# Packed attention and SwiGLU on one core: in the later batches, one output product ahead of M and the attention products

## The chip, the cores and the metric

The kernel runs on one core of one Trainium2 chip. The metric is device time in microseconds (us) of one execution. Engines are named as in the profile: PE is the TensorE with its matmuls, PEld its weight loads, DVE the VectorE, ACT the ScalarE, POOL the GpSimd, SP the queue that issues the DMAs.

## The reference

Two attentions in a row, of which the second has the output of the first as keys and values, and then a gated feed-forward layer over all tokens. There are 8 batches, 8 heads, 576 positions, 64 elements a head, 32 packed rows, model width 512 and inner width 1536.

```python
def sm_attn(qq, kk, vv):
    s = scale * np.matmul(qq, kk.transpose(0, 1, 3, 2))
    s = s - np.max(s, axis=-1, keepdims=True)
    a = np.exp(s)
    a = a / (np.sum(a, axis=-1, keepdims=True) + 1e-09)
    return np.matmul(a, vv)
p_packed = sm_attn(p, k, v)
out = sm_attn(q, p_packed, p_packed)
...
g = x @ w_gate              # x: out, as 4608 tokens x 512
silu = g * (1.0 / (1.0 + np.exp(-g)))
val = x @ w_val
return (silu * val @ w_out).astype(np.float32)
```

## The kernel before

The kernel doesn't form x. The second attention's weights a2 (tokens by 32 packed rows of each head) are multiplied by M, which is the packed output of the first attention times w_gate and w_val. M is made anew for each batch, in parts of two chunks of the inner width; a chunk is 128 of its 1536 columns, so there are 12 chunks (`fc` 0 to 11) in a batch. Each factor of these products, and of the output product, is split into a high and a low part (`mh`/`ml`, `a2h`/`a2l`, `hh`/`hl`, `wo_h`/`wo_l`), and three of the four products of parts are added up in PSUM.

The first batch follows a written program of its own. The later batches (b = 1 to 7) go through `batch(b, behind)`. A chunk there does this on PE: gate/value of its first half (256 tokens), the output products of the preceding chunk's first half, gate/value of its second half (320 tokens), the output products of the preceding chunk's second half. Gate/value (`gv_chunk`, L655) is 12 matmuls, six into each of two PSUM banks; ACT reads the first bank (silu, L662) and DVE the second (L666, and L669 for 64 tokens that are kept apart), then the product is split (`hh`, `hl`). An output product (`out_mm`, L674) is three matmuls of 512 columns into one of four accumulators. A half has two of them (`c` = 0 and 1, for 128 tokens each).

PE's order is the order in which the program is written. `fill`, called after each bank of gate/value and after each output product, counts up in the chunk, and `run(fc, place)` issues what a table has for that place: the next batch's attention, piece by piece. At count 2, when gate/value of the first half is issued, a chunk of odd number also issues a part of M (`m_part`, L274 into two `aux` banks). The pieces at place "ha" come right after: the first attention's scores (`q_scores`, L416), its packed product (`q_pack`, L500) or the second attention's scores (`s2_mm`, L274 with `q_t`). These go into the pool `gv`, which has two banks and is the pool of gate/value too, so the next gate/value takes the banks that they leave. DVE reads them: the scores by a maximum and a subtraction a bank (L431, L432), the packed product by eight small transposes (L512), the second attention's scores by one transpose a bank (L533). Behind those reads DVE makes `hl` (L636) and the low parts of M (L593).

The odd chunks of batches 1 to 6 carry scores in chunk 1, pack in 5, second scores in 7 and 9, and, in batches 1 to 5, scores again in 11. Chunk 3 has M alone, as have chunk 11 of batch 6 and the odd chunks of batch 7 up to 9.

DVE, ACT and SP follow the order that a scheduler finds, except for instructions that are pinned to the order of the program.

Of the kernel before, what the change touches and what calls it, by code (L numbers as in the profile page):

```python
# [20 lines left out]
B, H, S, D = 8, 8, 576, 64  # L21
NP = 32
DM, DF = 512, 1536
P = 128
NPAR, NHP = 2, 4
NFC = DF // P
# [108 lines left out]
def tile_pack_attention_swiglu(ctx: ExitStack, tc: tile.TileContext, qT, kT, v, vq, pT, wgv, wout, out):  # L135
# [96 lines left out]
    def wout_high(fc):  # L232
        k, i = divmod(fc, 2)
        if i == 0:
            wo_h[k], wo_l[k] = pair(F32R, "wo_h"), pair(F32R, "wo_l")
        pin(nc.scalar.copy(wo_h[k][:, i], wos[k][:, i]))

    def wout_low(fc):
        k, i = divmod(fc, 2)
        pin(nc.vector.tensor_tensor(wo_l[k][:, i], wos[k][:, i], wo_h[k][:, i].bitcast(F32), op=ALU.subtract))  # L240
# [350 lines left out]
    def m_lows():  # L591
        while lows:
            pin(nc.vector.tensor_tensor(*lows.pop(0), op=ALU.subtract))  # L593
# [29 lines left out]
    def m_part(b, k, fcs):  # L623
        m_mm(b, k, fcs)
        m_high(b, k, fcs)
# [6 lines left out]
    def h_split(src, hi, lo, between=lambda: False, tag=""):  # L632
        hh, hl = (pool.tile([P, 256], F32R, tag=t + tag, bufs=2, name=t) if tag else h_tile(t) for t in ("hh", "hl"))
        copy(hi, hh, src)
        last = between()
        low = lo.tensor_tensor(hl, src, hh.bitcast(F32), op=ALU.subtract)  # L636
        if last:
            pin(low)
        return hh, hl

    def gv_chunk(b, fc, is_b, fill, behind, between):
        odd = b % 2
        n = NB if is_b else NA
        off = (0 if odd else 256) if is_b else (320 if odd else 0)
        mh, ml = ms[b, fc // 2]
        ah, al = a2[b]
        f = fc % 2
        pgs = []
        for s in range(2):
            pg = ps_gv.tile([P, 512], F32, tag="gv", name="gv")  # L650
            pgs.append(pg)
            i = 0
            for m_, a_ in ((ml, ah), (mh, al), (mh, ah)):
                for g in range(NPAR):
                    nc.tensor.matmul(  # L655
                        pg[:, :n], m_[:, g, f, s * P : (s + 1) * P], a_[:, g, off : off + n],
                        start=(i == 0), stop=(i == 5),
                    )
                    i += 1
            fill()  # L660
        sg = pool.tile([P, NB], F32, tag="sg", bufs=1, name="sg")
        nc.scalar.activation(sg[:, :n], pgs[0][:, :n], AF.Silu)  # L662
        behind()
        hf = pool.tile([P, 256], F32, tag="hf", bufs=2, name="hf")
        o, o4 = (64, 0) if is_b and odd else (0, 256)
        nc.vector.tensor_tensor(hf, pgs[1][:, o : o + 256], sg[:, o : o + 256], op=ALU.mult)  # L666
        if is_b:
            r, r4 = slice(64 * odd, 64 * odd + 64), slice(o4, o4 + 64)
            nc.vector.tensor_tensor(t4[b // 2][:, fc, r], pgs[1][:, r4], sg[:, r4], op=ALU.mult)  # L669
        return h_split(hf, nc.scalar, nc.vector, between)  # L670

    def out_mm(acc, hh, hl, c, fc, at=slice(0, DM), first=False):
        for i, (h_, w_) in enumerate(((hl, wo_h), (hh, wo_l), (hh, wo_h))):
            nc.tensor.matmul(  # L674
                acc[:, at],
                h_[:, c : c + P],
                w_[fc // 2][:, fc % 2, at],
                start=((fc == 0 or first) and i == 0),
                stop=(fc == NFC - 1 and i == 2),
            )  # L680
# [58 lines left out]
    def plan_of(b):  # L739

        plan = {}
        for d in (b + 1, b + 2):
            if d >= B:
                continue
            for line in table_of(d).strip().splitlines():
                place, *todo = line.split()
                fc, place = place.split(".")
                fc = int(fc) + NFC * (d - b - 1)
                if (0 if d > 2 else -NFC) <= fc < NFC:
                    plan.setdefault((fc, int(place) if place.isdigit() else place), []).extend((words2[w], d) for w in todo)  # L750
        return lambda fc, place: bool([f(d) for f, d in plan.pop((fc, place), ())])

    with tc.manual_schedule(engines={mybir.EngineType.PE}):
# [8 lines left out]
        def accs_of(b):  # L762
            odd = b % 2
            row0 = (b // 2) * 2 * S
            rows = [row0 + P * t for t in ((7, 8, 5, 6) if odd else (0, 1, 2, 3))]
            return rows, [ps_acc.tile([P, 512], F32, tag="acc", name="acc") for _ in range(4)]

        def t4_of(b):
            t4[b // 2] = pool.tile([P, NFC * P + 48], F32, tag="t4", bufs=1, name="t4")[:, : NFC * P].rearrange(
                "p (f t) -> p f t", f=NFC  # L770
            )

        with tc.manual_schedule(
# [18 lines left out]
            rows, accs = [], []  # L792
# [133 lines left out]
        def last_outs(rows, accs, out):  # L926
            def last(which):
                out(which)
                for c in range(2 * which, 2 * which + 2):
                    emit_out(accs[c], rows[c], c % 2)  # L930

            return last
# [4 lines left out]
        def batch(b, behind):  # L937
            if not b % 2:
                t4_of(b)
            run = plan_of(b)  # L940
            ha, hb = {}, {}
            accs, rows = [], []

            def outs(fc, which, fill=lambda: None):
                src = (hb if which else ha).pop(fc)
                for c in range(2):
                    out_mm(accs[2 * which + c], *src, c * P, fc)
                    fill()

            for fc in range(NFC):  # L950
                count = [0]

                def fill():
                    count[0] += 1
                    if count[0] == 2:
                        run(fc, 2)
                        if fc == NFC - 1 and b + 1 < B:
                            m_part(b + 1, 0, both)
                        elif fc % 2 and fc + 1 < NFC:
                            m_part(b, (fc + 1) // 2, both)  # L960
                    if b == 1 and 1 <= fc <= 2 * SPLIT - 4 and count[0] == 7:
                        wout_high(fc + 3)
                        wout_low(fc + 3)
                    if count[0] != 2:
                        run(fc, count[0])

                ha[fc] = gv_chunk(b, fc, False, fill, lambda: run(fc, "a"), lambda: run(fc, "ha"))
                m_lows()
                if fc:
                    outs(fc - 1, 0, fill)  # L970
                else:
                    behind(0)
                hb[fc] = gv_chunk(b, fc, True, fill, lambda: run(fc, "b"), lambda: run(fc, "hb"))
                if fc:
                    outs(fc - 1, 1, fill)
                else:
                    behind(1)
                    for x, y in zip((rows, accs), accs_of(b)):
                        x.extend(y)
            last = last_outs(rows, accs, lambda which: outs(NFC - 1, which))  # L980
            if not b % 2:
                return last
            p4, halves = [], {}

            def split4(*ks):
                for k in ks:
                    halves[k] = h_split(
                        t4_t[:, 2 * k : 2 * k + 2].rearrange("p f t -> p (f t)"), nc.vector, nc.vector, tag="4"
                    )

            def mm4(*ks):
                for k in ks:
                    for i in range(2):
                        out_mm(p4[0], *halves[k], i * P, 2 * k + i)

            def behind_p4(which):
                if which == 0:
                    p4.append(ps())
                    for k in range(4):
                        mm4(k)  # L1000
                        split4(k + 2)
                else:
                    row = (b // 2) * 2 * S + 4 * P
                    if b == B - 1:
                        mm4(4)
                        end_out(p4[0], row, halves[5])
                        return
                    mm4(4, 5)
                    emit_out(p4[0], row, 0)

            t4_t = t4.pop(b // 2)
            split4(0, 1)
            for which in range(2):
                last(which)
            return behind_p4

        for b in range(1, B):
            behind = batch(b, behind)
# [40 lines left out]
```

## Time and profile before

| | |
|---|---|
| median of 3 timed runs | 728.88 us (728.43 to 729.27) |
| span of the profiled execution (its own time, first to last instruction; the page has no other) | 727.1 us |
| the median over that span | 1.8 us |
| mean granted TensorE clock | 1.000 |
| PE gate/value, L655, on the chain that ended last | 37% |
| PE output products, L674 into `acc`, on that chain | 36% |
| M and the second attention's scores, L274 into `aux`, on that chain | 7% |

A row of the timeline gives start, duration, engine, line, operation and tiles (output<-inputs), the count of instructions that it merges, and in brackets the idle time of the engine ahead of it with what ended it. Durations of matmuls reach to a modelled end and overlap with the next one; the step from one start to the next tells what a matmul took of PE. A 32-bit matmul that isn't split stands in the trace as two, so M's 8 instructions are 16 rows and the scores' 16 are 32. Rows of waits give what waited, for whom, the total in us, how often, and the longest.

### The profile page before, as it was taken

What the parts mean: (1) busy time and instruction counts of PE and PEld (TensorE: products, weight loads), DVE (VectorE), ACT (ScalarE), POOL (GpSimd) and SP (SyncE); (2) the same over time, 40 slices, a digit from 0 to 9 for tenths busy, and PEclk for the clock granted to TensorE, in tenths of its full rate; (3) what the DMA queues carried; (4) which work ended last, traced back from release to release, by engine and by line L of the source; (5) the groups of instructions that cost most, each with busy time, mean ns of one, the idle gap of its engine ahead of it and who ended that gap; (6) DMA issues with size and microseconds to landing.
All of it is one profiled execution on the core that took longest, in us unless ns stands there. A gap on an engine that the chain in (4) does not pass through costs nothing.

```text
span 727.1 us, 14219 instructions
## 1 busy us (share of the span) xinstructions
PE 715.4 (98%) x5768; PEld 588.9 (81%) x5768; DVE 466.4 (64%) x1061; ACT 374.6 (52%) x675; POOL 2.0 (0%) x13
## 2 busy tenths in 40 slices
PE   6899999999999999999999999999999999999998
PEld 3656788888888888888888888888888888888886
DVE  5998999665745657565665566666574655744333
ACT  3889855734635355552653526653553535433331
POOL 0000000000000000000000000000000000000000
PEclk9999999999999999999999999999999999999999
DMA  9887293220212201302112021102001000010002
GB/s 356 313 301 280 94 372 108 89 73 1 67 72 72 74 1 66 128 3 73 66 59 85 3 73 67 59 4 73 1 2 73 5 1 1 1 60 1 1 1 73
DMA packets 20145, 59.10 MB, mean 81 GB/s; under 512 B 6000, under 2 KB 7280, under 8 KB 17520
## 3 DMA queue, kind: packets, MB, share of 16 engines
q1 hardware_dynamic: 19792, 57.96, 22.1%
q8 instruction: 46, 0.75, 0.4%
q10 hardware_dynamic: 288, 0.23, 0.1%
q14 instruction: 19, 0.16, 0.1%
HBM read 48.69 MB, written 9.49 MB: 80 GB/s over the span
## 4 chain that ended last, share of the span: by engine, by line
PE 96%; DVE 1%; ACT 0%; issue 0%; ACTq 0%; DVEq 0%
PE gv L655 37%; PE acc L674 36%; PE aux L274 7%; PE gv L821 6%; PE aux L674 5%; PE acc L862 3%; PE gv_aux L500 1%; PE gv_aux L274 1%; PE gv_aux L416 1%; PE acc L760 0%; PE aux L361 0%; DVE s L548 0%; DVE r L547 0%; PE gv_aux L361 0%; PE aux L342 0%; DVE s L533 0%
## 5 line engine op out<-in xcount | busy, mean ns | idle before, releaser
L662 ACT ACTIVATE sg<-gv 128x256 f32<-128x256 f32 (+1 forms) x168 | 69.1, 411 | 173.7 <-PE gv L655 161.6
L666 DVE TENSOR_TENSOR hf<-gv,sg 128x256 f32<-128x256 f32 x168 | 70.8, 422 | 120.0 <-PE gv L655 108.4
L674 PE MATMUL acc<-wo_h,hl 128*128 128x512 f32 x360 | 146.5, 407 | 0.0
L655 PE MATMUL gv<-a2h,ml 128*128 128x256 f32 (+1 forms) x672 | 143.7, 295 | 0.0
L655 PE MATMUL gv<-a2l,mh 128*128 128x256 f32 (+1 forms) x672 | 143.4, 295 | 0.0
L655 PE MATMUL gv<-a2h,mh 128*128 128x256 f32 (+1 forms) x672 | 143.4, 295 | 0.0
L674 PE MATMUL acc<-wo_l,hh 128*128 128x512 f32 x360 | 141.8, 394 | 0.0
L674 PE MATMUL acc<-wo_h,hh 128*128 128x512 f32 x360 | 141.8, 394 | 0.0
L655 PEld LDWEIGHTS gv<-a2h,ml 128*128 128x128 f32 x672 | 116.3, 189 | 15.1
L185 ACT CAST hh<-hf 128x256 fp32r<-128x256 f32 x168 | 67.7, 403 | 104.0 <-DVE hf L666 103.9
L655 PEld LDWEIGHTS gv<-a2l,mh 128*128 128x128 f32 x672 | 107.7, 189 | 0.1
L655 PEld LDWEIGHTS gv<-a2h,mh 128*128 128x128 f32 x672 | 107.6, 188 | 0.0
L636 DVE TENSOR_TENSOR hl<-hf,hh 128x256 fp32r<-128x256 f32 x168 | 70.0, 417 | 46.3 <-ACT hh L185 45.9
L674 PEld LDWEIGHTS acc<-wo_h,hl 128*128 128x128 f32 x360 | 67.5, 188 | 30.4 <-issue 20.3
L674 PEld LDWEIGHTS acc<-wo_h,hh 128*128 128x128 f32 x360 | 67.6, 188 | 15.3
L674 PEld LDWEIGHTS acc<-wo_l,hh 128*128 128x128 f32 x360 | 67.7, 188 | 8.7 <-ACT mh L619 0.2
L593 DVE TENSOR_TENSOR ml<-aux,mh 128x512 fp32r<-128x512 f32 x92 | 58.9, 681 | 3.7 <-ACT mh L619 3.4
L274 PE MATMUL aux<-w,ppt 64*32 64x512 f32 (+1 forms) x784 | 52.1, 588 | 0.0
L619 ACT CAST mh<-aux 128x512 fp32r<-128x512 f32 x92 | 49.4, 590 | 5.0 <-PE aux L274 0.5
L662 ACT ACT_TABLE_LOAD x30 | 38.5, 1283 | 14.0 <-PE gv L655 9.5
L205 ACT ACTIVATE st<-st,minus_two 128x1024 f32<-128x1024 uint32 x18 | 22.6, 1264 | 0.0
L862 PE MATMUL acc<-wo_f,h 128*128 128x512 f32 x48 | 22.5, 601 | 0.0
(158 smaller groups left out, 743.8 us busy)
## 6 DMA issues: line engine op xcount, KB each, us to landing
st<-in_wgv SPq DMA_DIRECT2D x12, 1024.0 KB, 6.5
k_t<-in_kT SPq DMA_DIRECT2D x16, 576.0 KB, 4.8
q_t<-in_qT SPq DMA_DIRECT2D x16, 576.0 KB, 5.0
out<-ot SPq DMA_DIRECT2D x35, 256.0 KB, 2.1
v_t<-in_vq SPq DMA_DIRECT2D x6, 1280.0 KB, 5.8
st<-in_wout SPq DMA_DIRECT2D x6, 1024.0 KB, 6.2
v_t<-in_v SPq DMA_DIRECT2D x2, 1024.0 KB, 8.3
p_t<-in_pT SPq DMA_DIRECT2D x7, 64.0 KB, 2.4
```

What stands on the lines that cost most here:

```text
L185: e.copy(dst, src)
L205: yield nc.scalar.activation(lo.bitcast(F32), lo.bitcast(U32), AF.Identity, bias=minus_two, scale=LOW_WORD)
L274: nc.tensor.matmul(outs[par][32 * hp : 32 * hp + 32], lhs(r, hp), rhs(r, hp), start=True, stop=True)
L593: pin(nc.vector.tensor_tensor(*lows.pop(0), op=ALU.subtract))
L619: nc.scalar.copy(m[0][at], src)
L636: low = lo.tensor_tensor(hl, src, hh.bitcast(F32), op=ALU.subtract)
L655: nc.tensor.matmul(pg[:, :n], m_[:, g, f, s * P : (s + 1) * P], a_[:, g, off : off + n], start=(i == 0), stop=(i == 5),)
L662: nc.scalar.activation(sg[:, :n], pgs[0][:, :n], AF.Silu)
L666: nc.vector.tensor_tensor(hf, pgs[1][:, o : o + 256], sg[:, o : o + 256], op=ALU.mult)
L674: nc.tensor.matmul(acc[:, at], h_[:, c : c + P], w_[fc // 2][:, fc % 2, at], start=((fc == 0 or first) and i == 0), stop=(fc == NFC - 1 an ...
L821: nc.tensor.matmul(held[i][s][:, :n], m_[:, g, f, s * P : (s + 1) * P], a_[:, g, off : off + n], start=(j == 0), stop=(j == len(todo) - 1),)
L862: nc.tensor.matmul(accs[2 * is_b + c], half(i)[:, c * P : c * P + P], wos[fc // 2][:, fc % 2], start=(fc == 0), stop=(fc == NFC - 1),)
```

## The change

In an odd chunk, once gate/value of the first half is issued and before M, the first of the two output products of the preceding chunk's first half is issued (`c` = 0, into `accs[0]`). It is noted in `early`, and `outs` leaves it out where it stood. M and the attention pieces at "ha" follow, then the second output product, then gate/value of the second half as before. The last chunk of the last batch is left as it was. That is 41 places: 6 in each of batches 1 to 6 and 5 in batch 7.

```diff
+            early = set()
+
             def outs(fc, which, fill=lambda: None):
                 src = (hb if which else ha).pop(fc)
                 for c in range(2):
-                    out_mm(accs[2 * which + c], *src, c * P, fc)
+                    if (fc, which, c) not in early:
+                        out_mm(accs[2 * which + c], *src, c * P, fc)
                     fill()
...
                     if count[0] == 2:
                         run(fc, 2)
+                        if fc % 2 and (fc + 1 < NFC or b + 1 < B):
+                            early.add((fc - 1, 0, 0))
+                            out_mm(accs[0], *ha[fc - 1], 0, fc - 1)
                         if fc == NFC - 1 and b + 1 < B:
                             m_part(b + 1, 0, both)
                         elif fc % 2 and fc + 1 < NFC:
```

PE at chunk 1 of a batch, before (`gv` is gate/value, `aux<-w` is M, `gv_aux<-k_t` the scores, `acc` the output products):

```order
L655 MATMUL gv<-a2h,mh 128x256 x2
L274 MATMUL aux<-w_82,ppt 32x512 x8
L416 MATMUL gv_aux<-k_t,p_t 32x144 x16
L674 MATMUL acc<-wo_h,hl 128x512
L674 MATMUL acc<-wo_l,hh 128x512
L674 MATMUL acc<-wo_h,hh 128x512
L674 MATMUL acc<-wo_h,hl 128x512
L674 MATMUL acc<-wo_l,hh 128x512
L674 MATMUL acc<-wo_h,hh 128x512
L655 MATMUL gv<-a2h,ml 128x320 x2
```

The same place on PE now:

```order
L655 MATMUL gv<-a2h,mh 128x256 x2
L674 MATMUL acc<-wo_h,hl 128x512
L674 MATMUL acc<-wo_l,hh 128x512
L674 MATMUL acc<-wo_h,hh 128x512
L274 MATMUL aux<-w_82,ppt 32x512 x8
L416 MATMUL gv_aux<-k_t,p_t 32x144 x16
L674 MATMUL acc<-wo_h,hl 128x512
L674 MATMUL acc<-wo_l,hh 128x512
L674 MATMUL acc<-wo_h,hh 128x512
L655 MATMUL gv<-a2h,ml 128x320 x2
```

Three matmuls of an output product moved ahead of M and the scores; three instead of six stand between the scores and gate/value's second half.

PE at chunk 5, before (`gv_aux<-v_t` is the packed product):

```order
L655 MATMUL gv<-a2h,mh 128x256 x2
L274 MATMUL aux<-w_84,ppt 32x512 x8
L500 MATMUL gv_aux<-v_t,a_1643 32x64 x40
L674 MATMUL acc<-wo_h,hl 128x512
L674 MATMUL acc<-wo_l,hh 128x512
L674 MATMUL acc<-wo_h,hh 128x512
L674 MATMUL acc<-wo_h,hl 128x512
L674 MATMUL acc<-wo_l,hh 128x512
L674 MATMUL acc<-wo_h,hh 128x512
L655 MATMUL gv<-a2h,ml 128x320 x2
```

The same place on PE now:

```order
L655 MATMUL gv<-a2h,mh 128x256 x2
L674 MATMUL acc<-wo_h,hl 128x512
L674 MATMUL acc<-wo_l,hh 128x512
L674 MATMUL acc<-wo_h,hh 128x512
L274 MATMUL aux<-w_84,ppt 32x512 x8
L500 MATMUL gv_aux<-v_t,a_1643 32x64 x40
L674 MATMUL acc<-wo_h,hl 128x512
L674 MATMUL acc<-wo_l,hh 128x512
L674 MATMUL acc<-wo_h,hh 128x512
L655 MATMUL gv<-a2h,ml 128x320 x2
```

Here too one output product went ahead of M and the packed product, and one stayed behind it.

ACT, SP and POOL keep their order. On DVE a few neighbours change places; the one that recurs is in chunk 3, shown as a difference (`ml` are M's low parts, `y`, `x` and `z` the first attention's maxima and sums):

```order
 L636 TENSOR_TENSOR hl<-hf,hh 128x256
-L593 TENSOR_TENSOR ml<-aux,mh 128x512 x2
-L460 TENSOR_REDUCE y_1555<-x_1487 128x8
-L461 TENSOR_TENSOR y_1555<-x_1487,y_1555 128x32
-L464 TENSOR_TENSOR y_1555<-z_1273,y_1555 128x8
+L593 TENSOR_TENSOR ml<-aux,mh 128x512
+L460 TENSOR_REDUCE y_1558<-x_1487 128x8
+L593 TENSOR_TENSOR ml<-aux,mh 128x512
+L461 TENSOR_TENSOR y_1558<-x_1487,y_1558 128x32
+L464 TENSOR_TENSOR y_1558<-z_1273,y_1558 128x8
```

The small maximum now stands between the two low parts of M instead of behind them.

## The prediction

> **What bounds the kernel now.** I read the page's busy and clock rows first, then the waits of PE (the TensorE), then the waits of DVE (the VectorE) that the change touches, and last the timeline around the moved products. Two lines of the page:
>
> ```profile
> PE 715.4 (98%) x5768; PEld 588.9 (81%) x5768; DVE 466.4 (64%) x1061; ACT 374.6 (52%) x675; POOL 2.0 (0%) x13
> PEclk9999999999999999999999999999999999999999
> ```
>
> PE fills 98% of the span, at an undisturbed clock. Busy PE says little by itself, since ends of matmuls are modelled, so the waits decide. All that PE's own view of the waits lists is this (what waited, for whom, us in total, times, longest):
>
> ```profile
> PE acc_aux L274 <- DMA p_t<-in_pT: 4.9, 1, 4.9
> PE gv L821 <- DVE a2f L790: 1.3, 1, 1.3
> PE gv L821 <- ACT mh L619: 0.8, 1, 0.8
> PE gv_aux L361 <- DMA v_t<-in_v: 0.7, 1, 0.7
> PE gv L821 <- ACT sg L837: 0.5, 1, 0.5
> ```
>
> Each belongs to the first batch's program (L821, L361, L274 on the first load). In the later batches, where the change acts, PE is never listed as waiting. So there is nothing for a reordering of PE to recover there, unless a wait hides in a matmul's duration; every slip of a result that PE needs soon can only cost. Who reads the moved products, and how ready it is, is in the waits of DVE:
>
> ```profile
> DVE s L533 <- PE gv_aux L274: 12.8, 12, 1.1
> DVE z L431 <- PE gv_aux L416: 11.6, 11, 1.1
> DVE ppt L512 <- PE gv_aux L500: 10.7, 6, 1.8
> ```
>
> DVE stands idle over 1 us in front of every attention product and starts when PE ends it. If PE ends it later, DVE starts later by as much. The counts give the sites: 11 of scores (L416), 6 of pack (L500), 12 of the second attention product (L274 with q_t), all in chunks of odd number. A further 12 odd chunks have M alone.
>
> **The score sites.** Timeline of PE and DVE at chunk 1 of a middle batch (start, duration, engine):
>
> ```profile
> 388.57 0.40 PE L655 MATMUL gv<-a2h,mh 128*128 128x256 f32 x2
> 388.90 1.09 PE L274 MATMUL aux<-w,ppt 64*32 64x512 f32 x16
> ...
> 389.78 0.75 PE L416 MATMUL gv_aux<-k_t,p_t 64*32 64x144 f32 x32
> ...
> 390.46 0.50 PE L674 MATMUL acc<-wo_h,hl 128*128 128x512 f32 x1
> 390.80 0.40 PE L674 MATMUL acc<-wo_l,hh 128*128 128x512 f32 x1
> 391.03 0.40 PE L674 MATMUL acc<-wo_h,hh 128*128 128x512 f32 x1
> 391.06 0.46 DVE L432 TENSOR_TENSOR e<-gv_aux,z 128x288 f32<-128x288 f32 x1
> 391.26 0.40 PE L674 MATMUL acc<-wo_h,hl 128*128 128x512 f32 x1
> ...
> 391.91 0.46 DVE L432 TENSOR_TENSOR e<-gv_aux,z 128x288 f32<-128x288 f32 x1
> 391.95 0.46 PE L655 MATMUL gv<-a2h,ml 128*128 128x320 f32 x2
> ...
> 392.84 0.45 PE L655 MATMUL gv<-a2h,ml 128*128 128x320 f32 x2
> ```
>
> One output product is three matmuls: the second one runs from 391.26 to the start of gate/value's second half at 391.95, 0.69 us. The first, now ahead of M, pushes M and the scores back by 0.69 and leaves only the second between the scores and gate/value. The work of PE up to gate/value is unchanged, so without waits gate/value would still be due at 391.95. But the scores use both banks of the two-bank gv pool, and gate/value needs the first of them back. DVE gives it back at 391.06 + 0.46 = 391.52, 0.43 before it is due. Slipped by 0.69 that is 392.21, 0.26 too late, and a bank given back isn't used at once: for that time the pack site has the row.
>
> **The pack sites.** Pack takes one bank, which gate/value needs for its second bank, half-way through:
>
> ```profile
> 418.07 2.06 DVE L512 STREAM_TRANSPOSE ppt<-gv_aux 32x64 f32<-32x64 f32 x8 [1.81 <-PE gv_aux L500]
> ...
> 420.02 0.46 PE L655 MATMUL gv<-a2h,mh 128*128 128x320 f32 x2
> 420.31 0.50 PE L655 MATMUL gv<-a2h,ml 128*128 128x320 f32 x2
> 420.65 0.46 PE L655 MATMUL gv<-a2l,mh 128*128 128x320 f32 x2
> ```
>
> Eight transposes end at 418.07 + 2.06 = 420.13, and the matmul that needs their bank starts 0.18 later, exactly when it is due (pairs follow each other by 0.29). The next pair then starts 0.34 later instead of 0.29: the bank came just in time, and 0.05 was lost since the second weight load was late too. So pack has no slack at all. I take 0.18 as the time from release to matmul, and 0.05 as the extra after a wait.
>
> Price per pack site: the whole slip, 0.69 (its 0.05 is paid already). Six of them: 4.1 us. Price per score site: 0.69 + 0.18 - 0.43 = 0.44, with the 0.05 it is 0.49; eleven: 5.4 us. The second bank adds nothing: it is free at 391.91 + 0.46 + 0.69 + 0.18 = 393.24, and with the wait it is due at 392.84 + 0.49 = 393.33. The lower bound, a bank used as soon as it is released, is 0.26 a site, 2.9 in all.
>
> **The second attention product.** Here DVE needs one transpose per bank, from the group's mean 463 ns; after it come M's low halves, a maximum (L547) and the multiplication that ends gate/value (L666, L669):
>
> ```profile
> L533 DVE STREAM_TRANSPOSE s<-gv_aux 128x288 f32<-128x288 f32 x26 | 11.1, 463 | 13.2 <-PE gv_aux L274 12.8 <-PE acc_aux L274 0.4
> ```
>
> ```profile
> 431.74 0.85 DVE L533 STREAM_TRANSPOSE s<-gv_aux 128x288 f32<-128x288 f32 x2 [1.06 <-PE gv_aux L274]
> ...
> 432.82 1.28 DVE L593 TENSOR_TENSOR ml<-aux,mh 128x512 fp32r<-128x512 f32 x2
> ...
> 433.07 0.46 PE L655 MATMUL gv<-a2h,ml 128*128 128x320 f32 x2
> ...
> 434.01 0.74 DVE L547 TENSOR_REDUCE r<-s 128x18 f32<-128x576 f32 x1
> ...
> 435.10 0.43 DVE L666 TENSOR_TENSOR hf<-gv,sg 128x256 f32<-128x256 f32 x1 [0.35 <-PE gv L655]
> ...
> 436.11 0.22 DVE L669 TENSOR_TENSOR t<-gv,sg 128x64 f32<-128x64 f32 x1
> 436.22 0.40 PE L655 MATMUL gv<-a2h,ml 128*128 128x256 f32 x2
> ...
> 436.93 0.40 PE L655 MATMUL gv<-a2h,ml 128*128 128x256 f32 x2
> ```
>
> The first bank is free at 431.74 + 0.46 = 432.20; with slip and latency 433.07, exactly when it is due. I take 0 and keep 0.07 a site (0.8 in all) for the upper end. DVE itself stays 0.69 late here, as PE didn't wait: L547 ends at 434.01 + 0.74 + 0.69 = 435.44, so L666 starts 0.34 late, and L669 frees its bank at 436.33 + 0.34 + 0.18 = 436.85, against 436.93. Covered, by 0.08; that cover is thin, and what it costs if gone is a rival below.
>
> **What costs nothing.** M alone (12 sites): no gv bank is read there, and M's low halves, ready at 432.82 + 1.28 = 434.10 even at the crowded site, have until the next chunk at 436.22; that slack of 2.1 also covers the small maximum (L460) that now stands between the two of them in chunk 3 of some batches. The product moved forward needs the low half of the chunk before. It is latest ahead of chunk 11:
>
> ```profile
> 455.44 0.42 DVE L636 TENSOR_TENSOR hl<-hf,hh 128x256 fp32r<-128x256 f32 x1
> ...
> 457.33 0.66 PE L274 MATMUL aux<-w,ppt 64*32 64x512 f32 x8
> ```
>
> It is there at 455.86, and the place where M stands now comes at 457.33: 1.4 to spare. DMAs keep their order on SP, and POOL's clearing of e is issued as before; the sums whose maxima SP gathers stand a chunk later, by when DVE has waited for PE again.
>
> **The boundary in front of M.** PE changes from full 128-row products to 64-row ones once per site, before as after, but behind a 512-wide matmul instead of a 256-wide one. Before: last 256-wide start 388.69 (388.57 + 0.12), M 388.90: 0.21, that is 0.09 over the usual 0.12. A wider one stands in the first batch:
>
> ```profile
> 80.24 0.46 PE L821 MATMUL gv<-a2h,ml 128*128 128x320 f32 x2
> ...
> 80.63 0.66 PE L274 MATMUL aux<-w,ppt 64*32 64x512 f32 x8
> ```
>
> The second of the pair starts at 80.39 (spacing 0.15), M 0.24 later: again 0.09 over. So it doesn't depend on the width: 0.
>
> **Sum.** 5.4 + 4.1 = 9.5 us on the profiled execution's span of 727.1: 736.6. The timed runs' median, 728.88, lies 1.8 above that span; with the same margin 738.4. Bounds of the costs: 2.9 + 4.1 = 7.0 and 9.5 + 0.8 = 10.3, so 735.9 to 739.2 if the mechanism holds.
>
> **Rivals.**
> DVE's lag bites at the second product. If L548, which stands between L666 and L669, delays the release by the full slip of 0.69 instead of 0.34, the bank comes 0.27 late, 12 times: 3.2 us more, 741.6. Against it: L666 had 0.35 of idle time that absorbs half the slip.
>
> The boundaries get cheaper (the other side). M's 0.09 might belong to the narrow product in front of it, and the slow start of the first output product behind the tiles (390.46 to 390.80, 0.34, where the next step, 390.80 to 391.03, takes 0.23: 0.11) might go as well. Both gone at 41 sites would give back 0.20 x 41 = 8.2, leaving 1.3: 730.2, within noise. It decides from 0.23 a site. Only the first half gone: 3.7, 734.7. For it: the order in front of M really changes. Against it: the 320-wide row above, and the second output product still comes right behind tiles.
>
> PE's clock drops because PE now stops 17 times.
>
> ```profile
> 20.00:25.00 5.00, 3.69 (x19) 2.98 (x18) 4.92 (x9) 4.01 (x7) 0.00 (x0) 1.00 0.91 366
> ```
>
> ```profile
> 23.49 0.45 PE L821 MATMUL gv<-a2f,mh 128*128 128x256 f32 x1 [1.31 <-DVE a2f L790]
> ```
>
> The granted clock (1.00 in the first row) stayed full over a gap of 1.31 us, longer than any stop here, so I give it little. If the gate/value half behind each stop (1.76 us, the 0.88 from 391.95 to 392.84 twice) ran at half clock, it would add 17 x 1.76 = 30: 768. The Trainium skill ("TensorE: Matmul & The Clock Gate", section "A second HAM failure mode: psum-queue depth-cycling") tells of a kernel whose short idle times between groups, while cycling through PSUM banks, made the clock oscillate; the row above doesn't show it here.
>
> The change does nothing: the slip is smaller than 0.25 at the scores only if PE starts M under the first output product. M's start after the last full product, 0.09 late, speaks against that. It would leave 728.9.
>
> **Chances.** Mechanism as summed 0.79; DVE's lag on top 0.08; boundary rival 0.06, half of it to no change and half to 734.7; the change does nothing 0.01; clock 0.03; faster by something unseen 0.03, since PE's waits could be hidden in modelled ends. Slower 0.93, same 0.04, faster 0.03, with 0.2% (1.5 us) as what a measurement can tell. The range 735.2 to 741.7 takes in the lag rival and the bounds.
>
> **What would show it.** Right: PE waits listed on DVE's L432 (11, some 0.4 each) and L512 (6, some 0.7), in front of L655, or first matmuls of that line later by as much; DVE's idle time in front of the three readers grows by what PE gained; the first 512-wide pair to M some 0.31 apart. Wrong: no gap at gate/value behind scores and pack, M starting closer than 0.25 behind the wide product, or a clock row below 1.00. The forecast fails if readers start before PE ends the product, or if the release takes effect faster than 0.18.

## The result, and the profile after

| | median | lowest to highest |
|---|---|---|
| before, timed again beside it | 729.00 us | 728.43 to 729.27 |
| after | 739.56 us | 738.40 to 739.93 |

The change costs 10.6 us: ratio 1.0139, 95% interval 1.0123 to 1.0156. The profiled execution of after took 739.9 us, its span is 738.1 against 727.1, and its page's busy and clock rows are these:

```profile
PE 719.5 (97%) x5768; PEld 578.8 (78%) x5768; DVE 463.2 (63%) x1061; ACT 375.0 (51%) x675; POOL 2.0 (0%) x13
PEclk9999999999999999999999999999999999999999
```

PE has as many matmuls as before, at the same clock, and does them in a longer span. Its waits say where it stopped:

```profile
PE gv L655 <- DVE ppt L512: 3.0, 6, 0.5
PE gv L655 <- DVE e L432: 2.6, 11, 0.2
...
PE acc L674 <- DVE hl L636: 0.4, 1, 0.4
```

The first two are the pack and the score sites, with just the counts that the sites have. The third is new and was not forecast. The totals (3.0 + 2.6 + 0.4 = 6.0) are less than the time lost: busy matmuls reach to a modelled end, past the start of their successor. What a stop cost is the step between starts, so I compare, matmul by matmul, when PE started the same one before and after. Here are the first and the last rows of gate/value in the later batches, before:

```profile
118.04 0.40 PE L655 MATMUL gv<-a2h,ml 128*128 128x256 f32 x2
...
710.91 0.45 PE L655 MATMUL gv<-a2h,mh 128*128 128x320 f32 x2
```

and after:

```profile
119.05 0.40 PE L655 MATMUL gv<-a2h,ml 128*128 128x256 f32 x2
...
721.92 0.46 PE L655 MATMUL gv<-a2h,mh 128*128 128x320 f32 x2
```

The first starts 1.01 later, the last 11.01. So 10.0 us arise in the later batches, where the change is. The other 1.0 arises in the first batch's program, in which PE's order is the same in both. In the ten profiled experiments below this first start lay between 117.41 and 119.38 us, without relation to what was changed: that is scatter from execution to execution. From here on "the late part" is the time between these two rows, compared with that of before. It repeats far better than a span: the version of experiment 4, whose later batches lost nothing, comes out within 0.1 us of before.

DVE (the VectorE) waited longer in front of all three readers, at every site:

```profile
DVE s L533 <- PE gv_aux L274: 21.1, 12, 1.8
DVE z L431 <- PE gv_aux L416: 19.2, 11, 1.8
DVE ppt L512 <- PE gv_aux L500: 14.9, 6, 2.5
```

That is 8.3, 7.6 and 4.2 us more than before, 0.69 or 0.70 a site: the slip, at all three kinds. Only two of them made PE wait.

**A score site after** (batch 4, chunk 1; PE, DVE's reads, and the weight load ahead of gate/value; here and below `...` stands for rows of PE and DVE that are left out):

```profile
395.83 0.39 PE L674 MATMUL acc<-wo_h,hh 128*128 128x512 f32 x1
396.15 1.09 PE L274 MATMUL aux<-w,ppt 64*32 64x512 f32 x16
397.03 0.75 PE L416 MATMUL gv_aux<-k_t,p_t 64*32 64x144 f32 x32
...
397.82 0.46 DVE L431 TENSOR_REDUCE z<-gv_aux 128x2 f32<-128x288 f32 x1 [1.76 <-PE gv_aux L416]
...
398.29 0.40 PE L674 MATMUL acc<-wo_h,hh 128*128 128x512 f32 x1
398.31 0.46 DVE L432 TENSOR_TENSOR e<-gv_aux,z 128x288 f32<-128x288 f32 x1
...
398.89 0.30 PEld L655 LDWEIGHTS gv<-a2h,ml 128*128 128x128 f32 x2 [0.65 <-issue]
398.92 0.53 PE L655 MATMUL gv<-a2h,ml 128*128 128x320 f32 x2 [0.23 <-DVE e L432]
...
399.29 0.45 PE L655 MATMUL gv<-a2l,mh 128*128 128x320 f32 x2
```

The last matmul of the output product starts at 398.29, so gate/value is due at 398.52. DVE gives the bank back at 398.31 + 0.46 = 398.77, and the matmul starts 0.15 after that, at 398.92: 0.40 late. The step to the next pair is 0.37, where before has 0.30 (391.95 to 392.25): another 0.07, and 0.07 to 0.08 over all sites. That goes with the weight loads (PEld). The one in front of gate/value starts 0.03 ahead of its matmul here, so the load of the pair's second matmul is late as well. Before, it started 0.22 ahead of the matmul at 391.95:

```profile
391.73 0.42 PEld L655 LDWEIGHTS gv<-a2h,ml 128*128 128x128 f32 x2
```

**A pack site after** (batch 4, chunk 5):

```profile
425.80 2.06 DVE L512 STREAM_TRANSPOSE ppt<-gv_aux 32x64 f32<-32x64 f32 x8 [2.50 <-PE gv_aux L500]
...
427.06 0.45 PE L655 MATMUL gv<-a2h,mh 128*128 128x320 f32 x2
...
428.01 0.53 PE L655 MATMUL gv<-a2h,ml 128*128 128x320 f32 x2 [0.50 <-DVE ppt L512]
```

The pair for the second bank is due 0.29 after 427.06, at 427.35. The transposes end at 427.86 and it starts at 428.01, again 0.15 later: 0.66 late, and 0.69 with the load that follows. The site had next to no slack, so it pays the whole slip.

**The second attention product after** (chunk 7 of batch 4):

```profile
440.16 0.85 DVE L533 STREAM_TRANSPOSE s<-gv_aux 128x288 f32<-128x288 f32 x2 [1.75 <-PE gv_aux L274]
...
440.57 0.40 PE L674 MATMUL acc<-wo_h,hh 128*128 128x512 f32 x1
440.81 0.46 PE L655 MATMUL gv<-a2h,ml 128*128 128x320 f32 x2
...
443.09 0.41 DVE L666 TENSOR_TENSOR hf<-gv,sg 128x256 f32<-128x256 f32 x1
...
444.66 0.40 PE L655 MATMUL gv<-a2h,ml 128*128 128x256 f32 x2
```

DVE waited 1.75 here instead of 1.06, PE didn't: gate/value follows the output product by 0.24, without a bracket. L666 has lost its idle time and starts 2.28 behind gate/value instead of 2.03, so DVE is 0.25 late (0.34 was forecast), and the next chunk's second bank (444.66) still doesn't wait.

**The stop that was not forecast**, at the end of batch 1. Before:

```profile
201.75 0.42 DVE L636 TENSOR_TENSOR hl<-hf,hh 128x256 fp32r<-128x256 f32 x1 [0.83 <-ACT hh L185]
...
202.09 0.68 DVE L187 COPY ot<-acc 128x512 f32<-128x512 f32 x1
...
202.36 0.40 PE L674 MATMUL acc<-wo_h,hl 128*128 128x512 f32 x1
```

and after:

```profile
204.50 0.69 DVE L187 COPY ot<-acc 128x512 f32<-128x512 f32 x1 [0.73 <-PE acc L674]
...
205.11 0.42 DVE L636 TENSOR_TENSOR hl<-hf,hh 128x256 fp32r<-128x256 f32 x1
205.58 0.50 PE L674 MATMUL acc<-wo_h,hl 128*128 128x512 f32 x1 [0.44 <-DVE hl L636]
```

The copy of a finished accumulator and the low half `hl` have changed places on DVE. The copy waits for PE's last output product into that accumulator; the input of `hl` was there earlier, but `hl` now stands behind the copy, and PE's next output product waits for `hl`. By starts it costs 0.69, once.

So the late part adds up, all by starts in this trace: 11 score sites x 0.48 = 5.3, 6 pack sites x 0.69 = 4.2, batch 1's end 0.69, all else -0.2: together 10.0.

### The profile page after: what moved, and what is told of

Same layout as the page of the kernel before. It is cut to its first block, busy times and chain, and to the rows that moved or that the text cites. A ratio compares the mean times of both kernels' runs of the same rounds, so it can differ in the third digit from the quotient of the medians.

```text
span 738.1 us, 14219 instructions
## 1 busy us (share of the span) xinstructions
PE 719.5 (97%) x5768; PEld 578.8 (78%) x5768; DVE 463.2 (63%) x1061; ACT 375.0 (51%) x675; POOL 2.0 (0%) x13
## 4 chain that ended last, share of the span: by engine, by line
PE 85%; DVE 4%; issue 1%; ACT 0%; DVEq 0%
PE gv L655 36%; PE acc L674 33%; PE aux L274 6%; PE aux L674 4%; PE gv L821 2%; DVE ppt L512 2%; PE gv_aux L500 1%; PE gv_aux L416 1%; PE gv_aux L274 1%; DVE e L432 1%; DVE z L431 1%; PE acc L862 0%; PE aux L361 0%; DVE wo_f L207 0%; DVE w L208 0%
## 5 line engine op out<-in xcount | busy, mean ns | idle before, releaser
L655 PE MATMUL gv<-a2h,ml 128*128 128x256 f32 (+1 forms) x672 | 144.6, 297 | 5.6 <-DVE ppt L512 3.0
L655 PE MATMUL gv<-a2h,mh 128*128 128x256 f32 (+1 forms) x672 | 143.4, 295 | 0.0
L655 PE MATMUL gv<-a2l,mh 128*128 128x256 f32 (+1 forms) x672 | 143.4, 295 | 0.0
L666 DVE TENSOR_TENSOR hf<-gv,sg 128x256 f32<-128x256 f32 x168 | 70.5, 420 | 106.2 <-PE gv L655 95.8
L655 PEld LDWEIGHTS gv<-a2h,ml 128*128 128x128 f32 x672 | 114.6, 189 | 26.5 <-issue 7.1
L655 PEld LDWEIGHTS gv<-a2l,mh 128*128 128x128 f32 x672 | 107.7, 189 | 0.1
L655 PEld LDWEIGHTS gv<-a2h,mh 128*128 128x128 f32 x672 | 107.7, 188 | 0.0
L533 DVE STREAM_TRANSPOSE s<-gv_aux 128x288 f32<-128x288 f32 x26 | 11.1, 464 | 21.5 <-PE gv_aux L274 21.1
L274 PEld LDWEIGHTS aux<-w,ppt 64*32 64x32 f32 x784 | 8.9, 104 | 18.0 <-issue 16.1
```

Source lines behind the costliest of these rows:

```text
L274: nc.tensor.matmul(outs[par][32 * hp : 32 * hp + 32], lhs(r, hp), rhs(r, hp), start=True, stop=True)
L533: pin(nc.vector.transpose(st2[b][0][:, c, par], two[b, c][par][:, :HS]))
L655: nc.tensor.matmul(pg[:, :n], m_[:, g, f, s * P : (s + 1) * P], a_[:, g, off : off + n], start=(i == 0), stop=(i == 5),)
```

## The experiments

Every version is timed against before on the same chip. Where nothing else is said, a version starts from the changed kernel; where it says "DVE held", it has the copy at the end of batch 1 kept behind `hl`.

**1. The exchange on DVE, undone** (`e1_hl`): the changed kernel, with DVE held.

```diff
-        copy(nc.scalar if eng else nc.vector, ot, acc)
+        if hold[0] and not eng:
+            with tc.issue_after(low_of[0].ins):
+                copy(nc.vector, ot, acc)
+        else:
+            copy(nc.scalar if eng else nc.vector, ot, acc)
...
+            hold[0] = b == 1
             for which in range(2):
                 last(which)
+            hold[0] = False
```

> The changed kernel, with DVE made to issue the low half of the last chunk of batch 1 ahead of the copy of an accumulator, as before the change. Theory (bank waits at scores and pack, 5.3 and 4.1 us, and besides them 0.7 us by this one exchange of neighbours on DVE): 0.7 us less than the changed kernel's 739.6, so 738.9, and PE's wait of 0.44 us on L636 at the end of batch 1 is gone from the waits. Rival (the exchange is chance and the 0.7 us lies in the order of PE there): 739.6, with the gap still there.

Measured: 737.99 us against 728.50, ratio 1.0130 (1.0116 to 1.0144). That interval overlaps after's, so the time alone doesn't tell 0.7 us. The trace does. Its PE waits in the later batches are

```profile
PE gv L659 <- DVE ppt L512: 3.0, 6, 0.5
PE gv L659 <- DVE e L432: 2.6, 11, 0.2
```

(L659 is L655 of after; four lines were added ahead of it). The wait on `hl` is gone, and the late part is +9.35 instead of +10.01. The exchange cost 0.66 to 0.69.

**2 to 4. One kind of site at a time**: pack alone, scores alone (DVE held), and the 24 others alone, which are M alone and M with the second attention product.

```diff
-if fc % 2 and (fc + 1 < NFC or b + 1 < B):
+if fc == 5 and b + 1 < B:                            # e2_pack
+if fc == 1 and b + 1 < B or fc == 11 and b + 2 < B:  # e3_score
+if fc in (3, 7, 9) or b + 1 == B and fc in (1, 5) or b + 2 == B and fc == 11:  # e4_rest
```

> The kernel before, with the output product moved ahead of M at the 6 pack sites (chunk 5) alone. Theory (the bank of the packed product comes back 0.69 us late): 729.0 + 6 x 0.69 = 733.1. Rival (each of the 41 moved products costs the same share of the 10.5 us, 0.26 us, whatever follows it): 729.0 + 6 x 0.26 = 730.5.

> The kernel before, with the output product moved at the 11 score sites (chunks 1 and 11) alone, DVE's order as before. Theory (the scores' first bank comes back 0.43 us late and the next weight load is late by 0.05): 729.0 + 11 x 0.48 = 734.3. Rival (an equal share per moved product, 0.26 us): 729.0 + 11 x 0.26 = 731.9.

> The kernel before, with the output product moved at the remaining 24 places alone: the 12 second attention products and the 12 places with M alone. Theory (no bank is late there): 729.0, PE without a wait in the later batches. Rival (equal share, 0.26 us each, or a dearer boundary in front of M): 729.0 + 24 x 0.26 = 735.2.

Measured:

| | median | before | ratio (95%) | late part |
|---|---|---|---|---|
| pack | 732.78 | 728.50 | 1.0061 (1.0047 to 1.0075) | +4.15 |
| scores | 733.61 | 728.50 | 1.0071 (1.0059 to 1.0084) | +5.24 |
| the others | 728.54 | 728.50 | 1.0002 (0.9993 to 1.0010) | -0.08 |

An equal share per moved product, the rival of all three, would have cost 1.6, 2.9 and 6.2 us. The intervals allow 3.4 to 5.5, 4.3 to 6.1 and -0.5 to 0.7, so it is excluded each time. Each of the first two versions lists the one wait that belongs to it, pack and then scores:

```profile
PE gv L655 <- DVE ppt L512: 3.0, 6, 0.5
```

```profile
PE gv L659 <- DVE e L432: 2.6, 11, 0.2
```

The third version lists none in the later batches. Yet its DVE waits as long in front of the second product's transposes as in after:

```profile
DVE s L533 <- PE gv_aux L274: 21.1, 12, 1.8
...
DVE z L431 <- PE gv_aux L416: 11.6, 11, 1.1
```

A DVE that waits 0.69 longer at 12 places costs nothing there: the late reader is paid for only where the bank is needed before the slip is over. The three late parts add up to 9.31, and with DVE held the whole change has 9.35: the sites don't influence each other. The third version also decides against cheaper boundaries in front of M, which would have shown at its 24 sites.

**5. A smaller slip** (`e5_third`, DVE held): only the first of the three matmuls goes ahead of M, the other two stay.

```diff
-out_mm(accs[0], *ha[fc - 1], 0, fc - 1)
+out_mm(accs[0], *ha[fc - 1], 0, fc - 1, part=(0,))   # parts 1 and 2 where it stood
```

> The changed kernel with only the first of the three matmuls of the output product moved ahead of M at the 41 places, DVE's order as before the change. The slip is 0.23 us instead of 0.69. Theory (a bank is late only by what the slip exceeds its slack, 0.27 at scores, nothing at pack): scores 0, pack 6 x 0.23 = 1.4, so 728.5 + 1.4 = 729.9. Rival (cost in proportion to what is moved): a third of the 9.4 us without DVE's exchange, 3.1, so 731.6.

Measured: 730.60 against 728.59, ratio 1.0031 (1.0019 to 1.0044), late part +1.94. The time (+2.0, 1.4 to 3.2 by the interval) lies nearer the slack theory but doesn't exclude the proportional rival. The trace does: no wait at any of the 11 score sites, where a slip of 0.23 fits into the slack, and 0.23 at each of the 6 pack sites (0.20 in front of the second bank, 0.03 at the load that follows), which is 1.4 and what the slack theory gave. The remaining 0.5 is spread over the other places at 0.01 to 0.02 each, without a wait. This small term was in neither expectation, and its cause isn't shown; the pack sites, where the output product is cut in two as well, don't have it.

**6. A larger slip** (`e6_both`, DVE held in every odd batch): both output products ahead of M, so nothing is left between the readers and gate/value.

```diff
-early.add((fc - 1, 0, 0))
-out_mm(accs[0], *ha[fc - 1], 0, fc - 1)
+for c in range(2):
+    early.add((fc - 1, 0, c))
+    out_mm(accs[c], *ha[fc - 1], c * P, fc - 1)
```

> The changed kernel with both output products of the first half moved ahead of M at the 41 places, low half and copy on DVE held in the old order. The slip is 1.39 us. Theory (slip less slack, and 0.07 for the late weight load): scores 11 x (1.39 - 0.27 + 0.07) = 13.1, pack 6 x 1.39 = 8.3, second attention product, which now waits too, 12 x (1.39 - 0.68 + 0.05) = 9.1; 728.5 + 30.5 = 759. Rival (in proportion to what is moved): twice 9.4, so 747.3.

Measured: 756.39 against 728.59, ratio 1.0376 (1.0362 to 1.0389), late part +27.4. PE's waits in the later batches:

```profile
PE gv L659 <- DVE e L432: 12.5, 11, 1.1
PE gv L659 <- DVE s L533: 7.6, 12, 0.6
...
PE gv L659 <- ACT sg L666: 4.7, 7, 1.2
```

By starts: scores 1.17 each, 12.9 in all (13.1 expected); the second attention product, free until now, 0.69 each, 8.3 in all (9.1 expected). So the slip passes its slack there too. Pack misses: 0.80 each, 4.8 in all, where 1.39 each was expected. The rows at a pack site tell why:

```profile
435.99 2.06 DVE L512 STREAM_TRANSPOSE ppt<-gv_aux 32x64 f32<-32x64 f32 x8 [3.19 <-PE gv_aux L500]
...
437.11 0.44 ACT L666 ACTIVATE sg<-gv 128x320 f32<-128x320 f32 x1 [1.27 <-PE gv L659]
437.60 0.56 PE L659 MATMUL gv<-a2h,ml 128*128 128x320 f32 x2 [0.59 <-ACT sg L666]
```

Gate/value's second bank starts at 437.60, 0.45 before the transposes end, and right behind the silu that read the first bank: in this version it takes the first bank again, not pack's. Which bank a tile gets came out differently with the new order (why, no run shows), so a slip can't be scaled past that point. DVE's order changed too: M's low parts stand later at several places. One more stop, 1.4 us in chunk 4 of batch 1, is a silu that stands later on ACT. Through some 30 stops the clock stayed at 1.00.

**7. The distance given back** (`e7_refill`, DVE held in every odd batch): after's early product stays, and at the score and pack sites the first output product of the second half is taken forward into the gap, so six matmuls stand between the readers and gate/value again.

```diff
 # behind the outs of the first half
+if fc in (1, 5) and b + 1 < B or fc == 11 and b + 2 < B:
+    early.add((fc - 1, 1, 0))
+    out_mm(accs[2], *hb[fc - 1], 0, fc - 1)
```

> The changed kernel, but at the score and pack sites the first output product of the second half is taken ahead of gate/value's second half, so that two products stand between the attention product and gate/value again; low half and copy on DVE held in the old order. Theory (what counts is the work of PE between the attention product and the gate/value that takes its bank): the waits go, up to 0.2 us at each pack site where M's low halves now come just in time for the next chunk; 728.5 + 0 to 1.2, so about 729. Rival (the late start of M and of DVE's reads is itself the cost): still 738, as without the refill.

Measured: 732.23 against 728.59, ratio 1.0051 (1.0038 to 1.0065). That is neither theory's number, but the mechanism holds: no wait on L432 or L512 is left, and 0.69 more in front of gate/value is 0.69 less behind it. New waits took the place:

```profile
PE acc L678 <- DVE hl L638: 1.1, 3, 0.4
...
PE gv L659 <- ACT sg L666: 0.7, 3, 0.3
```

The first are the ends of batches 1, 3 and 5 (0.69 each by starts): the output product used as filler in chunk 11 had been the cover for `hl` there. Two of the second kind cost 0.48 each in chunk 0 of batches 3 and 5, one 0.55 in chunk 2 of batch 1. Together that is 3.6, against a late part of 3.45.

**8. The distance alone** (`e8_packmore`): before's order, nothing ahead of M, but the same filler at the pack sites.

> The kernel before, with nothing moved ahead of M, but at the 6 pack sites the first output product of the second half taken ahead of gate/value's second half: three products instead of two behind pack. Theory: the 0.05 us that the kernel before loses at each pack site goes, 0.3 us in all, 728.2, too little to be told from 728.5. Rival (gate/value's second half, now later against DVE's work, delays the next chunk): slower by 0.2 us or more a site, 729.7 or above.

Measured: 728.30 against 728.59, ratio 0.9994 (0.9986 to 1.0003): no difference in time. In the trace each pack site takes 0.69 more and the place behind it 0.74 less, and the late part is -0.39. The 0.05 of a late weight load that before's row showed at pack is there to be had, and six of them are too little to time.

**9. Refill without chunk 11** (`e9_refill`, DVE held in every odd batch): nothing is moved in chunk 11; elsewhere the early product with its filler. The expectation also leaves chunk 1 of batch 1 out; the kernel that ran did move and fill it, so it has 35 places, not 34.

```diff
-if fc % 2 and (fc + 1 < NFC or b + 1 < B):
+if fc % 2 and fc + 1 < NFC:
...
+if fc in (1, 5) and b + 1 < B:
+    early.add((fc - 1, 1, 0))
+    out_mm(accs[2], *hb[fc - 1], 0, fc - 1)
```

> The output product moved ahead of M at 34 of the 41 places (not in chunk 11 and not in chunk 1 of batch 1), and at the 5 score and 6 pack sites among them the first output product of the second half taken ahead of gate/value's second half; low half and copy on DVE in the old order. Theory (two products between attention product and gate/value are enough, wherever M starts): no wait at these sites, 728.6 + 0 to 0.5, about 728.8. Rival (the late start of M, of the attention product and of DVE's reads costs by itself): 5 x 0.47 + 6 x 0.69 = 6.5 more, 735.1.

Measured: 729.28 against 728.70, ratio 1.0010 (1.0001 to 1.0019), late part +0.43. All but one of the 0.69 are given back, and that one is the place that the expectation had left out:

```profile
PE gv L659 <- ACT sg L666: 0.3, 1, 0.3
```

It costs 0.55 by starts, in chunk 2 of batch 1. At the other 11 score and pack sites, with the distance restored, the early product is as free as at the sites that never cost anything.

**10. The late reader without the moved product** (`e10_late`, DVE held): before's order on PE. DVE takes the first bank's maximum three times instead of once at the 11 score sites (a repetition that changes no value), so the bank comes back two maxima late.

```diff
-            pin(nc.vector.tensor_reduce(m, x, axis=AX.X, op=ALU.max))
+            for _ in range(3 if par == 0 and (b > 2 or g == 1) else 1):
+                pin(nc.vector.tensor_reduce(m, x, axis=AX.X, op=ALU.max))
```

> The kernel before, with PE's order untouched, but at the 11 score sites DVE computes the maximum of the first bank three times instead of once (the two extra ones are repeats without effect), so that bank comes back some 0.87 us later. Theory (PE waits for the bank alone): 11 x (0.87 - 0.27 + 0.07) = 7.4, so 736.0, with PE waiting on L432 in the profile. Rival (the order of PE's products makes the cost, not the bank): 728.6, unchanged, since DVE has idle time there.

Measured: 737.09 against 728.70, ratio 1.0116 (1.0100 to 1.0131), late part +8.3. Its rows (line numbers are one or more higher here):

```profile
PE gv L660 <- DVE e L433: 5.8, 11, 0.5
```

```profile
396.34 0.40 PE L679 MATMUL acc<-wo_h,hh 128*128 128x512 f32 x1
396.66 0.46 DVE L433 TENSOR_TENSOR e<-gv_aux,z 128x288 f32<-128x288 f32 x1
...
397.26 0.53 PE L660 MATMUL gv<-a2h,ml 128*128 128x320 f32 x2 [0.52 <-DVE e L433]
```

The matmul is due at 396.34 + 0.23 = 396.57 and starts at 397.26, 0.69 late, with 0.14 from the release at 397.12. Two more maxima brought the bank back 0.98 later (three together took 1.44, one takes 0.46; the expectation had 0.87). Before, it was back 0.43 ahead of time: 0.98 - 0.43 + 0.14 is the 0.69, and with the late load of 0.07 it is 0.76 at each of 11 sites. PE's order was untouched: what costs is the late release, however it comes about.

## Why the prediction was right

- **Scores**, 11 x 0.49 = 5.4: measured 0.48 each, 5.3, and 5.24 alone. The working held, but two of its terms were off. The 0.18 from release to matmul was 0.15: it came from a row of the pack site whose matmul started just when it was due, so that row gives an upper bound and not the time itself. The 0.05 for the late load was 0.07 to 0.08. That the two errors cancel is luck. Experiment 3 shows the term by itself, experiment 10 shows its cause without the change.
- **Pack**, 6 x 0.69 = 4.1: measured 4.2, and 4.15 alone. The slip is the price, and a third of the slip cost a third (0.23, experiment 5). "No slack at all" was off by the same 0.03 (0.18 less 0.15): the matmul comes 0.66 late, and the load behind it brings the price to 0.69.
- **The second attention product**, 0: held. Experiment 4 shows it, and experiment 6 that its cover ends where the slip is doubled. The rival with DVE's lag was wrong: L666's delay was absorbed.
- **M alone and the boundary in front of M**, 0: held. After a 512-wide matmul M starts 0.32 later (395.83 to 396.15), 0.09 over the usual 0.23, as forecast from the first batch. Nothing was given back there, so the rival on the other side was wrong.
- **The clock**: full throughout. The Trainium skill ("TensorE: Matmul & The Clock Gate", "A second HAM failure mode: psum-queue depth-cycling") tells of a kernel whose clock oscillated since PE was idle briefly and often between groups of matmuls while it cycled through PSUM banks. No run here shows that: the 18 listed stops of after and the 30 of experiment 6 left the granted clock at 1.00.
- **The signs that it named**: the waits on L432 and L512 are there, 11 and 6 times; the list gives them as 0.2 and 0.5 instead of 0.4 and 0.7, the starts as 0.40 and 0.66. One sign against it came true without the forecast failing: the release took effect faster than 0.18. That alone lowers the price of a score site by 0.03, which the dearer load made up for.
- **What was missed**: the step that costed DVE's changed neighbours at nothing. It looked at the exchange in chunk 3 and not at the one at the end of batch 1, where a copy that waits for PE came ahead of the low half that PE waits for. It is worth 0.69 (experiment 1).
- **The margin**: the profiled span grew by 1.0 more than the late part, from the first batch's program. The forecast has no such term and needs none: it scatters. The measured 739.56 lies 1.2 above the forecast of 738.4. Of this, 0.5 is 10.0 instead of 9.5 in the later batches, and the rest is of the size of that scatter; the interval of the ratio takes in the forecast.

## What to carry to other kernels

Where a producer on PE hands PSUM banks to another engine and soon needs them back, the matmuls in between are the reader's time: moving them ahead of the producer is free only up to the slack read at that place (bank returned, plus 0.15 us here, against the start that is due), and costs the rest at every place. Refill the distance, or don't move; and look at what the refill had covered before. When code is moved on one engine, compare the order on the others to the end, because one exchange of a waiting copy with something that PE needs cost 0.69 us here.

## What had not been expected of the hardware

- The first batch's program, the same in every version on PE, ended anywhere from 117.4 to 119.4 us. A difference of less than 2 us between two single spans says nothing in this kernel; the time between two starts in its later batches resolves 0.1 us.
- With one of an output product's three matmuls moved ahead (experiment 5), the places that don't wait took 0.01 to 0.02 us more each. No run shows why.
- PE waits in the list understate the stop: 3.0 us for six stops at pack that cost 4.15 by starts, and 2.6 for eleven at scores that cost 5.24, since a matmul's modelled end reaches over the gap and the late weight load comes after it.
